# A fused attention and MLP kernel on one core: filler matmuls dealt to the first halves of slots, and one of them sent ahead of the maxima's products

## The chip, the core and the metric

The kernel runs on one core of one Trainium2 chip. A core has five engines that work side by side, each through its own queue in program order: TensorE (PE; its weight loads are shown apart as PEld), VectorE (DVE), ScalarE (ACT), GpSimd (POOL) and SyncE (SP), which here issues the DMAs. They wait for each other by semaphores. The metric is the device time of one execution in microseconds (us); less is better.

## The reference

The input x is 2048 rows of 512. It is normalised, and feeds a causal sliding-window attention (32 heads of 16, window 256) and an MLP whose SiLU gates the attention's output:

```python
xn = _layernorm(x, axis=-1)
s = _A_ref(xn, A_wqkv, A_wo)      # q, k, v; softmax(q k^T / 4 in the window) v; times wo
g = _silu(_B_ref(xn, B_w1, B_b1, B_w2, B_b2))   # layernorm, 1792 wide GELU layer, back to 512
return x + s * g
```

## The kernel before

**Layout and stages.** A preface normalises and transposes x and projects the first queries, keys and values. Then comes the attention, 128 *slots* t = 0 to 127: eight groups of four heads, and in each group 16 blocks of 128 keys. After it the rest of the MLP and the output projection follow, which the change does not touch. All matrix products in the projections are done with a high and a low part of each operand, three products in place of one.

**A slot.** The four heads of a group are kept as two pairs (p = 1 and p = 0). In slot t the loop at the end of the attention's code (from `for t in range(-16, end + 1)`) writes, in this order:

1. `prob_block(..., 1)`: scores of pair 1 into the bank pair `stb` (PE, two matmuls), exp into a tile `pt` (ACT), masks by POOL;
2. `max_block` for slot m = t + 12: products `xy` (PE, four matmuls), from which VectorE finds row maxima for a later group: a masked copy (COPY_PREDICATED) that takes parts of `zo` into `xy`, then a TENSOR_REDUCE into `mt`;
3. `fill_in(t, 0)`: the filler units of the first half;
4. `prob_block(..., 0)`: scores of pair 0 into the same `stb`, exp, masks;
5. `fill_in(t, 1)`: the filler units of the second half;
6. `first_scores` for slot m + 1: four matmuls into `zo`, which the next slot's masked copy reads (zo<-qk in the profile);
7. `closing`: where a tandem ends, ACT copies one finished bank out of PSUM, VectorE the other;
8. `pv_step`: products of exps and values (zo<-pt,vt), copied out by ACT (`oraw`).

Steps 1 to 3 are called the *first half* here, 4 to 8 the *second half*. Since there is one `stb`, the scores of either half wait for the exp of the half before. Slots 3 and 4 of each group of 16 have no first_scores, slot 5 has them with no wait for the copy; slots 14 and 15 of each 16 have narrower scores (256 and 128 columns in place of 384). In slots 1 and 2 of each 16, step 8 has 8 and 16 matmuls in place of 24.

**Fillers.** Between these steps PE does unrelated work: the projections of the next group's queries and keys, of the later heads' values (slots 51 to 73), and from slot 99 on the MLP's first layer. `tandem(t0, t1, one, two, mid)` spreads two such jobs over slots t0 to t1: a *unit* is two matmuls that run side by side on the halves of the array (64 rows each), one into `fb[0]`, one into `fb[1]`. A job pair takes 12 units of 512 columns in each of two phases (24 units of 256 columns for the values; `n` in the code, and `room` is counted in twelfths of it). `room(t, k)` says how many units half k of slot t holds, `places` deals them out. In slot t1 `closing` copies both banks out, ACT's copy and VectorE's, VectorE's behind the slot's reduction. The next tandem begins in slot t1 + 1 and its first matmul writes VectorE's bank. These are called *closing* slots (8, 13, 18, 24, 29, 34, 40, ...) and *starting* slots (9, 14, 19, 25, 30, 35, 41, ...). From slot 116 on `places_late` deals, which is left as it is. In slots 91 and 92 the fillers are transposes (`y_turn`).

Of the kernel before, what the change touches and what calls it, by code (L numbers as in the profile page):

```python
# [49 lines left out]
def mixer_kernel(ctx, tc, x, wqk, wv, wo, w1, b1, w2, b2, out):  # L50
# [106 lines left out]
    def run(steps):  # L157
        for step in steps:
            step()
# [11 lines left out]
    slots = []  # L171

    def open_slot(i):
        slots.append(bigp.tile([P, 2, 2, S], F32R, tag=f"qk{i}", name=f"qk{i}"))
# [122 lines left out]
    fills = {}  # L297
# [72 lines left out]
    def pair_qk(n, c):  # L370

        ops = [(kt, a, b) for kt in range(KT) for a, b in PASSES]
        sl = slice(512 * c, 512 * (c + 1))

        def mm(ps, i, r, **flags):
            kt, a, b = ops[i]
            nc.tensor.matmul(ps, wqs[n][r, a, kt], big[r, b, kt, sl], **flags)

        def send(src, qk, tt):
            copy_rows(slots[n % 2][tt:P:4, qk, :, sl], src[64 * qk: 64 * qk + 64])  # L380

        def finish(ps, t, copy):
            hi = sgp.tile([P, 512], F32R, tag="sh", name=f"sh_{n}_{c}", bufs=2)
            raw = t2.tile([P, 512], F32, tag="t2", name=f"pjr_{n}_{c}")
            lo = raw.bitcast(F32R)
            copy(raw, ps)

            def send_high():
                if n >= 2:
                    copy_rows(slots[n % 2][3:P:32, 0, :, sl], slots[n % 2][7:P:32, 0, :, sl])  # L390
                for qk, tt in ((1, 0), (0, 0), (1, 2), (0, 1)):
                    send(hi, qk, tt)

            def send_low():
                send(lo, 1, 1)
                send(lo, 0, 2)


            free = max(t + 1 + 2 * (c % 2), 16 * n - 28 + 4 * c)
            free += 2 * (t == 90)  # L400
            at(free, nc.scalar.copy, hi, raw)
            behind(free, send_high)
            free = quiet(max(free, t + 1))
            at(free, lambda: nc.gpsimd.tensor_tensor(lo, raw, hi.bitcast(F32), op=ALU.subtract))
            behind(free, send_low)
        return 3 * KT, mm, finish
# [37 lines left out]
    def tandem(t0, t1, one, two, mid=None, back=None):  # L444

        n = one[0]
        lo, hi = slice(0, 64), slice(64, P)
        mid = mid or max(1, (t0 + t1 + 1) // 2)  # L450
        late = t1 >= 16 * NQ - LEAD

        def room(t, k):

            m = t % 16
            if k:
                return {1: 2, 2: 1, 3: 1, 4: 1}.get(m, 0)
            return 3 if t == t0 else {5: 3, 15: 3}.get(m, 4)

        def places(slots, last):  # L460

            halves = [(t, k) for t in slots for k in (0, 1) if last or (t, k) != (mid - 1, 1)] + [(t1, 0)] * last
            units = dict.fromkeys(halves, 0)
            for _ in range(n - last * n // 12):
                h = min(units, key=lambda h: (units[h] >= room(*h) * n // 12, units[h]))
                units[h] += 1
            if last:
                units[t1, 1] = n // 12
            return [h for h in units for _ in range(units[h])]

        def places_late(slots, last):

            last = min(n // 4, n // (len(slots) + 1)) if last else 0
            cuts = [(n - last) * k // len(slots) for k in range(len(slots) + 1)]
            out = []
            for t, a, b in zip(slots, cuts, cuts[1:]):
                ahead = b - a if not last and t == slots[-1] else min(b - a, max(n // 4, (b - a + 1) // 2))
                out += [(t, 0)] * ahead + [(t, 1)] * (b - a - ahead)
            return out + [(t1, 0)] * last

        deal = places_late if late else places
        first, second = deal(range(t0, mid), False), deal(range(back or mid, t1), True)
        for phase, where in enumerate((first, second)):
            for i in range(n):
                flags = dict(start=(phase == 0 and i == 0), stop=(phase == 1 and i == n - 1), skip_group_check=True)
                def unit(i=i, phase=phase, flags=flags):
                    (two if phase == 0 else one)[1](fb[1 - phase], i, hi, **flags)
                    (one if phase == 0 else two)[1](fb[phase], i, lo, **flags)
                fills.setdefault(where[i], []).append((unit, ()))
        closing[t1] = (one[2], (fb[0], t1, nc.scalar.copy)), (two[2], (fb[1], t1, nc.vector.tensor_copy))  # L490
        if late:
            fills[t1, 0].extend(closing.pop(t1))
# [70 lines left out]
    def prob_block(n, kb, p):  # L563
        slot = slots[n % 2]
        w = min(384, S - P * kb)
        pt = pp.tile([P, 2, 384], F32, tag="pt", name=f"pt_{n}_{kb}_{p}")
        both = xy if p and 16 * n + kb + LEAD >= 16 * NQ else stb[0]
        for a in (1, 0):
            r = slice(64 * a, 64 * a + 64)
            nc.tensor.matmul(both[:, a, 0:w], slot[r, 1, p, P * kb: P * (kb + 1)],  # L570
                             slot[r, 0, p, P * kb: P * kb + w], start=True, stop=True)
        nc.scalar.activation(pt[:, :, 0:w], both[:, :, 0:w], AF.Exp, scale=DH ** -0.5)
        nc.gpsimd.affine_select(out=pt[:, :, 0:P], in_=pt[:, :, 0:P], pattern=[[0, 2], [1, P]],
                                compare_op=ALU.is_ge, fill=0.0, base=0, channel_multiplier=-1)
        if w == 384:
            nc.gpsimd.affine_select(out=pt[:, :, 256:384], in_=pt[:, :, 256:384],
                                    pattern=[[0, 2], [-1, P]], compare_op=ALU.is_gt, fill=0.0,
                                    base=0, channel_multiplier=1)
        pts[(n, kb, p)] = pt
# [100 lines left out]
    def at(t, fn, *args):  # L680
        plan.setdefault(t, []).append((fn, args))
# [71 lines left out]
    soon = {}  # L753
    tandem(3, 8, pair_qk(1, 2), pair_qk(1, 3))
    for n, spans in enumerate((((9, 13, 12), (14, 18, 17)), ((19, 24, 22), (25, 29, 28)), ((30, 34, 33), (35, 40, 38)),
                               ((41, 45, 44), (46, 50, 49)), ((74, 79, 77), (80, 84, 83)), ((85, 90, 88), (93, 98, 97))), 2):
        for c, span in zip((0, 2), spans):
            tandem(*span[:2], pair_qk(n, c), pair_qk(n, c + 1), *span[2:])
    for i, span in enumerate(((51, 56, 54), (57, 61, 60), (62, 67, 65), (68, 73, 71))):
# [61 lines left out]
    def fill_in(t, half):  # L821
        now[:] = t, half
        run(delayed.pop((t, half), ()))
        for fn, args in fills.get((t, half), ()):
            fn(*args)
# [3 lines left out]
    for t in range(-16, end + 1):  # L829
        m = t + LEAD  # L830
        if t == -5:
            open_slot(1)
            for k in range(4):
                at(-4 + k, clear_part, k)
        if 0 <= t < end:
            if t == 0:
                early.close()
                stb.append(attn.enter_context(tc.tile_pool(name="ps_s2", bufs=1, space=PSUM)).tile(
                    [P, 2, 512], F32, name="stb"))
            prob_block(t // 16, t % 16, 1)  # L840
        if t >= 0 and m < end:
            max_block(m // 16, m % 16, m in early_first)
        fill_in(t, 0)
        for fn, args in plan.get(t, []):
            fn(*args)
        if m == 1:
            max_block(0, 1)
        if 0 <= t < end:
            prob_block(t // 16, t % 16, 0)
        whole = t <= 2 or 91 <= t < 93  # L850
        if not whole:
            fill_in(t, 1)
        if t >= 0 and m + 1 < end and (m + 1) % 16 >= 2 and ((m + 1) % 4 or m >= 32):
            first_scores((m + 1) // 16, (m + 1) % 16)
            early_first.add(m + 1)
        if whole:
            fill_in(t, 1)
        if m == 0 or 1 <= m < LEAD - 1:
            max_block(0, m + (m > 0))
        for fn, args in closing.get(t, ()):  # L860
            fn(*args)
        if t >= 1:
            pv_step((t - 1) // 16, (t - 1) % 16)
        run(lns.get(t, ()))
        done = m if t >= 0 else m + 1 if 0 < m < LEAD - 1 else 0
        if done < end and done % 4 == 3:
            max_rows(done // 16, done % 16 // 4, t)
        for fn, args in ends.get(t, []):
            fn(*args)
# [20 lines left out]
    for f in range(6, NF, 2):  # L890
        t = gp.tile([P, 2, 512], F32, tag="ohl", name=f"hr_{f}", bufs=4)
# [185 lines left out]
    for c in range(2):  # L1077
# [23 lines left out]
        for i in range(NF + 1):  # L1101
# [47 lines left out]
            k = i - o_from  # L1149
# [163 lines left out]
```

## Time and profile before

| what | value |
|---|---|
| time, median of 3 runs | 750.82 us (750.6 to 752.12) |
| the profiled execution's own time | 750.51 us |
| its span on the core | 748.4 us |
| preface, attention, rest (from the timeline) | 0 to 64, 64 to 430, 430 to 748 us |
| granted TensorE clock over the span | 0.999 |

A slot takes about 2.8 us, and the attention's 128 slots half of the time. In the timeline's rows the first number is the start in us from the span's start, the second the duration, then the engine, the operation with what it writes and reads, the shapes, how many instructions are merged, and in brackets how long the engine stood idle before it and what ended that.

### The profile page before, as it was taken

The numbers are of one execution on the slowest core, as the hardware profiler recorded it, in microseconds if no ns is written. First come the engines' busy times: TensorE is split into PE (matmuls) and PEld (weight loads), VectorE is DVE, ScalarE is ACT, GpSimd is POOL, SyncE is SP. The second block draws the span as 40 slices with busy tenths as digits, with TensorE's granted clock in tenths as the row PEclk, the third lists the DMA queues.
The fourth block names the chain that finished last, engine by engine and source line by source line (L and its number), as shares of the span: only waits on it lengthen the run. The fifth ranks groups of instructions, "written<-read, shape, count | busy, mean of one in ns | idle before, by whom it ended". The sixth has DMA issues, their size and how long they took to land.

```text
span 748.4 us, 18785 instructions
## 1 busy us (share of the span) xinstructions
PE 737.2 (99%) x7412; PEld 589.7 (79%) x7412; DVE 502.5 (67%) x770; ACT 439.3 (59%) x745; POOL 314.8 (42%) x658
## 2 busy tenths in 40 slices
PE   9999999999999999999999999999999999999997
PEld 8886777777788887777776788888888888888886
DVE  8875667677677768787872648763576765676373
ACT  7756777777677666888877745454463744442001
POOL 7633777777566665867877600120102000001102
PEclk9999999999999999999999999999999999999999
DMA  8623365654348763547624482532013232253531
GB/s 284 196 61 79 73 155 146 164 141 99 95 111 250 242 220 85 134 109 201 198 76 148 136 286 94 194 122 87 26 48 103 91 99 72 69 178 120 171 95 56
DMA packets 56951, 99.40 MB, mean 133 GB/s; under 512 B 11104, under 2 KB 11360, under 8 KB 56864
## 3 DMA queue, kind: packets, MB, share of 16 engines
q1 hardware_dynamic: 56864, 98.21, 44.3%
q8 instruction: 58, 0.95, 0.5%
q14 instruction: 29, 0.24, 0.1%
HBM read 51.39 MB, written 29.62 MB: 108 GB/s over the span
## 4 chain that ended last, share of the span: by engine, by line
PE 81%; ACT 2%; DVE 1%; POOL 1%; DMA 1%; issue 1%; SPq 0%; ACTq 0%; DVEq 0%
PE acc L42 20%; PE fb L42 15%; PE zo L42 13%; PE p L42 9%; PE stb L42 9%; PE s L42 6%; PE h L42 6%; PE xy L42 3%; ACT pt L42 2%; POOL pt L42 1%; DMA qk<-mT_d 1%; PE yt L42 1%; DVE xy L42 0%; DVE mt L42 0%; SPq L42 0%
## 5 line engine op out<-in xcount | busy, mean ns | idle before, releaser
L42 POOL TENSOR_SCALAR_AFFINE_SELECT pt<-pt 128x256 f32<-128x256 f32 x480 | 189.8, 420 | 115.3 <-ACT pt L42 113.4
L42 ACT ACTIVATE pt<-stb 128x768 f32<-128x768 f32 (+1 forms) x244 | 188.6, 773 | 55.4 <-PE stb L42 47.8
L42 DVE TENSOR_REDUCE mt<-xy 128x4 f32<-128x1024 f32 (+1 forms) x128 | 152.6, 1192 | 4.4
L42 PE MATMUL acc<-w,gh 128*128 128x512 f32 x432 | 133.5, 390 | 0.0
L42 DVE COPY_PREDICATED xy<-upper,zo 128x512 f32<-128x512 int32 x112 | 77.9, 696 | 81.0 <-PE xy L42 65.8
L42 POOL TENSOR_TENSOR xo<-xo,gated 128x512 f32<-128x512 f32 x15 | 20.2, 1349 | 216.6 <-DVE gated L42 213.0
L42 PE MATMUL fb<-xnT,wqb 64*128 64x512 f32 (+1 forms) x684 | 108.2, 396 | 0.2
L42 PE MATMUL zo<-pt,vt 128*17 128x128 f32 x2880 | 103.7, 275 | 0.3 <-POOL pt L42 0.3
L42 PE MATMUL stb<-qk 64*128 64x384 f32 (+1 forms) x488 | 101.0, 409 | 2.9 <-ACT pt L42 1.3
L42 PEld LDWEIGHTS acc<-w,gh 128*128 128x128 f32 x432 | 80.8, 188 | 16.6
L42 PEld LDWEIGHTS stb<-qk 64*128 64x128 f32 x488 | 45.6, 183 | 54.8 <-ACT pt L42 46.4
L42 PE MATMUL acc<-w,gl 128*128 128x512 f32 x216 | 84.2, 390 | 0.0
L42 PEld LDWEIGHTS zo<-pt,vt 128*17 128x17 f32 x2880 | 67.5, 97 | 16.8 <-issue 7.5
L42 PEld LDWEIGHTS fb<-xnT,wqb 64*128 64x128 f32 (+1 forms) x684 | 64.9, 185 | 8.4 <-DVE pjr L42 0.8
L42 PE MATMUL xy<-qk 64*128 64x256 f32 (+2 forms) x536 | 58.2, 291 | 1.0 <-DVE mt L42 1.0
L42 ACT COPY oraw<-zo 128x128 f32<-128x128 f32 x128 | 34.3, 268 | 36.3 <-PE zo L42 35.0
L42 PEld LDWEIGHTS xy<-qk 64*128 64x128 f32 x536 | 46.8, 185 | 7.3 <-issue 3.3
L42 PEld LDWEIGHTS acc<-w,gl 128*128 128x128 f32 x216 | 40.5, 188 | 8.7 <-DVE gl L42 0.3
L42 ACT ACTIVATE gated<-acc 128x512 f32<-128x512 f32 x16 | 8.7, 596 | 63.5 <-DVE acc L42 63.5
L42 PE MATMUL s<-wos,ohl 128*128 128x512 f32 (+1 forms) x204 | 44.7, 377 | 0.0
L42 PEld LDWEIGHTS s<-wos,ohl 128*128 128x128 f32 x204 | 36.6, 188 | 7.0
L42 PEld LDWEIGHTS zo<-qk 64*128 64x128 f32 x448 | 38.4, 184 | 4.3 <-DVE xy L42 1.8
(198 smaller groups left out, 1169.2 us busy)
## 6 DMA issues: line engine op xcount, KB each, us to landing
qk<-sh SPq DMA_DIRECT2D x128, 128.0 KB
qk<-pjr SPq DMA_DIRECT2D x64, 128.0 KB
oT_d<-oraw SPq DMA_DIRECT2D x32, 256.0 KB
w_d<-in_w_dram SPq DMA_DIRECT2D x14, 512.0 KB
x<-in_x_dram SPq DMA_DIRECT2D x16, 256.0 KB
or<-oT_d SPq DMA_DIRECT2D x16, 256.0 KB
w<-rden_d SPq DMA_DIRECT2D x16, 256.0 KB
xo<-in_x_dram SPq DMA_DIRECT2D x16, 256.0 KB
```

The costliest lines, as they stand in the source:

```text
L42: r = issue(*args, **kwargs)
```

## The change

Three edits. `room` gives a first half four units (three in slot 15 of a group), also in a tandem's first slot, and a second half none but where it says 1 or 2. `places` fills the first halves before it puts anything into second halves, and takes the closing slot's two halves among them, where it used to set one unit aside for its second half. In the loop, where a slot's first half has more than one unit, its first unit is written ahead of `max_block`, so ahead of the xy products (slots 9 to 115, but for 91 and 92). One tandem's middle also moves from slot 97 to 96.

```diff
         def room(t, k):
 
             m = t % 16
-            if k:
-                return {1: 2, 2: 1, 3: 1, 4: 1}.get(m, 0)
-            return 3 if t == t0 else {5: 3, 15: 3}.get(m, 4)
+            return {1: 2, 2: 1, 3: 1, 4: 1, 15: 1}.get(m, 0) if k else {15: 3}.get(m, 4)
 
         def places(slots, last):
 
-            halves = [(t, k) for t in slots for k in (0, 1) if last or (t, k) != (mid - 1, 1)] + [(t1, 0)] * last
+            halves = [(t, k) for t in slots for k in (0, 1) if last or (t, k) != (mid - 1, 1)] + [(t1, 0), (t1, 1)] * last
             units = dict.fromkeys(halves, 0)
-            for _ in range(n - last * n // 12):
-                h = min(units, key=lambda h: (units[h] >= room(*h) * n // 12, units[h]))
-                units[h] += 1
-            if last:
-                units[t1, 1] = n // 12
-            return [h for h in units for _ in range(units[h])]
+            full = lambda h: units[h] >= room(*h) * n // 12
+            for _ in range(n):
+                units[min(halves, key=lambda h: (2, 1 - h[1], units[h]) if full(h) else (h[1], 0, units[h]))] += 1
+            return [h for h in halves for _ in range(units[h])]
...
-                               ((41, 45, 44), (46, 50, 49)), ((74, 79, 77), (80, 84, 83)), ((85, 90, 88), (93, 98, 97))), 2):
+                               ((41, 45, 44), (46, 50, 49)), ((74, 79, 77), (80, 84, 83)), ((85, 90, 88), (93, 98, 96))), 2):
...
             prob_block(t // 16, t % 16, 1)
+        if 9 <= t < 116 and t not in (91, 92) and len(fills.get((t, 0), ())) > 1:
+            fills[t, 0].pop(0)[0]()
         if t >= 0 and m < end:
             max_block(m // 16, m % 16, m in early_first)
         fill_in(t, 0)
```

How many units the halves hold, of tandems that stand for the rest (first half, second half of each slot):

| slots | before | now |
|---|---|---|
| 19 to 24 | 3,1 4,1 3,0 4,0 4,0 3,1 | 4,0 4,0 4,0 4,0 4,0 4,0 |
| 25 to 29 | 3,1 4,0 4,0 4,3 4,1 | 4,0 4,0 4,0 4,2 4,2 |
| 30 to 34 | 3,1 3,1 4,0 4,3 4,1 | 4,0 3,1 4,0 4,2 4,2 |
| 62 to 67 (half-size units) | 6,2 6,2 8,0 6,4 5,2 5,2 | 8,0 6,2 8,0 8,0 8,0 8,0 |
| 93 to 98 | 3,0 3,0 3,0 3,0 4,3 4,1 | 4,1 4,0 3,0 4,0 4,0 4,0 |

**PE's queue in slot 22**, in the middle of a tandem, before (zo<-qk are the first scores; then come the products with values):

```order
L42 MATMUL stb_890<-qk1_722 128x384 x2
L42 MATMUL xy_103<-qk0_92 128x256 x4
L42 MATMUL fb0_108<-xnT_90,wqb3_1619 128x512
L42 MATMUL fb1_109<-xnT_90,wqb3_1619 128x512
L42 MATMUL fb0_108<-xnT_90,wqb3_1619 128x512
```

and now:

```order
L42 MATMUL stb_890<-qk1_722 128x384 x2
L42 MATMUL fb0_108<-xnT_90,wqb3_1619 128x512
L42 MATMUL fb1_109<-xnT_90,wqb3_1619 128x512
L42 MATMUL xy_103<-qk0_92 128x256 x4
L42 MATMUL fb0_108<-xnT_90,wqb3_1619 128x512
```

One unit (a matmul into either bank) has moved from behind xy to ahead of it; three follow, as before. The second half is the same: stb, first scores, products.

**PE's queue from the second half of closing slot 24 into starting slot 25**, before, from stb on (the six rows of products with values between are left out by a line):

```order
L42 MATMUL stb_890<-qk1_722 128x384 x2
L42 MATMUL fb0_108<-xnT_90,wqb3_1619 128x512
L42 MATMUL fb1_109<-xnT_90,wqb3_1619 128x512
L42 MATMUL zo_104<-qk0_92 128x128 x4
...
L42 MATMUL stb_890<-qk1_722 128x384 x2
L42 MATMUL xy_103<-qk0_92 128x256 x4
L42 MATMUL fb1_109<-xnT_90,wqb3_1619 128x512
```

and now:

```order
L42 MATMUL stb_890<-qk1_722 128x384 x2
L42 MATMUL zo_104<-qk0_92 128x128 x4
...
L42 MATMUL stb_890<-qk1_722 128x384 x2
L42 MATMUL fb1_109<-xnT_90,wqb3_1619 128x512
L42 MATMUL fb0_108<-xnT_90,wqb3_1619 128x512
L42 MATMUL xy_103<-qk0_92 128x256 x4
```

The unit of the closing slot's second half is now in its first half, and the starting slot's first unit, whose first matmul writes fb1, stands ahead of xy.

**VectorE's queue over the same two slots**, the same before and now but for buffer numbers (mt are maxima, pjr a finished projection):

```order
L42 COPY_PREDICATED xy_103<-upper_115,zo_104 128x4x128
L42 TENSOR_REDUCE mt_2_4_2047<-xy_103 128x4
L42 STREAM_TRANSPOSE mT_2_0_2040<-mh_2_0_2037 128x32
L42 COPY pjr_3_1_2077<-fb1_109 128x512
L42 COPY_PREDICATED xy_103<-upper_115,zo_104 128x4x128
```

The copy that frees fb1 stands between the closing slot's reduction and the starting slot's masked copy. Nothing has moved here, nor on ACT, POOL or SP.

## The prediction

> **What bounds the kernel now.** I read the page first, for the shares and the chain that ended last.
>
> ```profile
> PE 737.2 (99%) x7412; PEld 589.7 (79%) x7412; DVE 502.5 (67%) x770; ACT 439.3 (59%) x745; POOL 314.8 (42%) x658
> ...
> PE 81%; ACT 2%; DVE 1%; POOL 1%; DMA 1%; issue 1%; SPq 0%; ACTq 0%; DVEq 0%
> ```
>
> TensorE looks full, but matmul ends are modelled and overlap, so its waits must be read from its weight loads (PEld). The view of waits for 85 to 400 us, which holds the slots that the change touches, names them:
>
> ```profile
> DVE xy L42 <- PE xy L42: 71.3, 88, 1.4
> ...
> PEld stb L42 <- ACT pt L42: 42.1, 160, 0.7
> ...
> PEld zo L42 <- DVE xy L42: 2.0, 7, 0.4
> ...
> PEld fb L42 <- DVE pjr L42: 1.2, 6, 0.3
> ...
> PEld xy L42 <- DVE mt L42: 0.4, 2, 0.2
> ```
>
> PE waits 160 times for an exp, hardly ever for the reduction ahead of an xy product (0.4 us in all), and VectorE waits 88 times for xy. So xy is late for VectorE, and VectorE is not late for xy. The timeline of slot 48 (four units in its first half, none in its second) shows why:
>
> ```profile
> 202.17 0.19 PEld L42 LDWEIGHTS stb<-qk 64*128 64x128 f32 x2 [0.21 <-issue]
> ...
> 202.45 0.40 PE L42 MATMUL xy<-qk 64*128 64x256 f32 x4
> ...
> 202.68 1.09 PE L42 MATMUL fb<-xnT,wqb 64*128 64x512 f32 x8
> 202.74 0.81 ACT L42 ACTIVATE pt<-stb 128x768 f32<-128x768 f32 x1 [0.17 <-PE stb L42]
> 202.95 0.70 DVE L42 COPY_PREDICATED xy<-upper,zo 128x512 f32<-128x512 int32 x1 [0.73 <-PE xy L42]
> ...
> 203.60 0.19 PEld L42 LDWEIGHTS stb<-qk 64*128 64x128 f32 x2 [0.26 <-ACT pt L42]
> 203.61 0.44 PE L42 MATMUL stb<-qk 64*128 64x384 f32 x2
> ...
> 203.68 1.23 DVE L42 TENSOR_REDUCE mt<-xy 128x4 f32<-128x1024 f32 x1
> 203.71 0.37 PEld L42 LDWEIGHTS zo<-qk 64*128 64x128 f32 x4
> ...
> 204.15 0.85 PE L42 MATMUL zo<-pt,vt 128*17 128x128 f32 x24
> ...
> 204.95 0.19 PEld L42 LDWEIGHTS stb<-qk 64*128 64x128 f32 x2 [0.23 <-ACT pt L42]
> ```
>
> The first half is 203.60 - 202.17 = 1.43 and ends with the exp, even with four units. The second is 204.95 - 203.60 = 1.35: first scores (zo<-qk) at 203.71, which may not overwrite zo before the masked copy (COPY_PREDICATED) has read it, at 202.95 + 0.70 = 203.65; then 24 products with V; then stb. So **two chains end together**: the exp's, and xy, masked copy, first scores, products, stb. The second has 0.06 us to spare. A unit takes (203.61 - 202.68)/4 = 0.23.
>
> **The change part by part.** All other engines' queues (ACT, DVE, POOL, SP) keep their order, so no copy, cast or DMA is moved past another, and nothing is added or removed. Only PE's order differs, in slots 3 to 115. I sum over these, against the profiled execution: span 748.4, own time 750.51, 0.3 under the median 750.82.
>
> *A. xy one unit later.* The masked copy follows xy directly (VectorE waited 0.73 for it), so it ends at 203.65 + 0.23 = 203.88 and first scores load at 203.93 instead of 203.71. What that costs, slot 54 shows, where the masked copy was late by itself:
>
> ```profile
> 220.24 0.70 DVE L42 COPY_PREDICATED xy<-upper,zo 128x512 f32<-128x512 int32 x1 [1.18 <-PE xy L42]
> ...
> 220.53 0.19 PEld L42 LDWEIGHTS stb<-qk 64*128 64x128 f32 x2
> ...
> 220.99 0.30 PEld L42 LDWEIGHTS zo<-qk 64*128 64x128 f32 x4 [0.27 <-DVE xy L42]
> ...
> 221.36 0.85 PE L42 MATMUL zo<-pt,vt 128*17 128x128 f32 x24
> ...
> 222.13 0.19 PEld L42 LDWEIGHTS stb<-qk 64*128 64x128 f32 x2 [0.21 <-issue]
> ```
>
> First scores load 0.05 after the copy's end; the products follow 0.37 behind, and stb 0.77 after that: 1.14 from load to stb. In slot 48 that gives 203.93 + 1.14 = 205.07, 0.12 to 0.13 later than 204.95. No other work covers it: PE has nothing between stb and first scores there. I count 22 slots that have no second-half unit afterwards and had none before: 22 x 0.13 = **+2.9**. (Slots of the V projection, 51 to 73, have half-size units and lose about nothing; slots 86, 102 and 103, whose masked copy was late anyway, nothing.) Between 0 and 0.23 a slot bounds it: 0 to 5.1.
>
> *B. Narrow slots.* In the last two slots of each group of 16 the scores are narrower, the exp shorter, and first scores already wait for the masked copy. Slot 31:
>
> ```profile
> 154.58 0.70 DVE L42 COPY_PREDICATED xy<-upper,zo 128x512 f32<-128x512 int32 x1 [0.70 <-PE xy L42]
> ...
> 155.33 0.30 PEld L42 LDWEIGHTS zo<-qk 64*128 64x128 f32 x4
> ...
> 156.48 0.19 PEld L42 LDWEIGHTS stb<-qk 64*128 64x128 f32 x2 [0.21 <-issue]
> ```
>
> 155.33 is 0.05 after the copy: the whole 0.23 passes on. Five such slots, one more with half-size units, and two of the other width: 7.5 x 0.23 = **+1.7**.
>
> *C. Units moved to first halves.* From closing slot 24 into starting slot 25, and from slot 28 (three units in its second half):
>
> ```profile
> 133.27 0.19 PEld L42 LDWEIGHTS stb<-qk 64*128 64x128 f32 x2 [0.21 <-ACT pt L42]
> ...
> 134.70 0.19 PEld L42 LDWEIGHTS stb<-qk 64*128 64x128 f32 x2 [0.49 <-ACT pt L42]
> ...
> 134.78 1.23 DVE L42 TENSOR_REDUCE mt<-xy 128x4 f32<-128x1024 f32 x1
> ...
> 136.05 0.65 DVE L42 COPY pjr<-fb 128x512 f32<-128x512 f32 x1
> 136.26 0.19 PEld L42 LDWEIGHTS stb<-qk 64*128 64x128 f32 x2 [0.21 <-ACT pt L42]
> ...
> 136.75 0.53 PEld L42 LDWEIGHTS fb<-xnT,wqb 64*128 64x128 f32 x6
> ...
> 137.69 0.19 PEld L42 LDWEIGHTS stb<-qk 64*128 64x128 f32 x2 [0.41 <-ACT pt L42]
> ...
> 139.25 0.19 PEld L42 LDWEIGHTS stb<-qk 64*128 64x128 f32 x2 [0.21 <-ACT pt L42]
> ```
>
> ```profile
> 146.19 0.19 PEld L42 LDWEIGHTS stb<-qk 64*128 64x128 f32 x2 [0.24 <-ACT pt L42]
> ...
> 148.20 0.19 PEld L42 LDWEIGHTS stb<-qk 64*128 64x128 f32 x2 [0.21 <-issue]
> ```
>
> A second half takes 1.35 with no unit, 1.56 with one (134.70 to 136.26), 2.01 with three. A first half of three units waits 0.49 for the exp, so a fourth there is free. One unit less saves 0.21, but A takes 0.13 back: slots 24, 40, 90, 104 gain 0.08 each; 56, 69, 73 (V units) 0.2 each, 58 0.1: **-1.0**. Ten slots go from three to two or fewer (-2.3), nine from one to two (+2.1): **-0.2**. Slot 3 now holds four units behind a late xy: **+0.2**.
>
> *D. Starting slots, the largest term.* The first unit of a tandem overwrites a bank that VectorE copies out behind its reduction in the closing slot: copy until 136.70, unit's load at 136.75. Until now xy went ahead of this wait; now xy waits in the queue behind the unit, and with it the other three units, stb, exp. Slot 25: the reduction and so the copy end 0.23 later, the closing slot gets 0.08 shorter, so the unit loads 0.49 + 0.31 = 0.80 into slot 25. A unit that was held costs more than 0.23, which slot 93 shows:
>
> ```profile
> 332.77 0.53 PEld L42 LDWEIGHTS fb<-xnT,wqb 64*128 64x128 f32 x6 [0.26 <-DVE xnT L42]
> ...
> 333.57 0.34 PE L42 MATMUL stb<-qk 64*128 64x384 f32 x2
> ```
>
> Three units in 0.80, so 0.34 for the held one. stb then comes at 0.80 + 0.34 + 0.23 (xy) + 3 x 0.23 = 2.06 instead of 1.43: +0.63; the second half goes from 1.56 to 1.48: net +0.55. By the same steps: slots 9, 25, 41, 57, 68, 74, 80, 99, 105 about 0.55 each (5.0); 14, 30, 46, 110 0.45 and 62 0.24, their closing slots being longer (2.0); 19, 35, 51 0.43 (1.3); 85 nothing, its closing slot growing with the copy's delay; 93, behind the transposes' copies, 0.8. Sum **+9.1**. Bounds: 0 if the wait does not hold xy back, 19 x 0.65 = 12.4.
>
> The Trainium skill, "TensorE: Matmul & The Clock Gate", section "The mechanism", says that weight loads may be pulled ahead but matmuls start and end strictly in program order. By that rule xy cannot pass the held unit, as D has it; were it otherwise, D would be 0. The rows above have no such case.
>
> Sum: 2.9 + 1.7 - 1.0 - 0.2 + 0.2 + 9.1 = 12.7. 750.5 + 12.7 = **763**.
>
> **The rivals.**
> *Only A to C.* The held unit turns out to cost little (the copy ends sooner, or stb is still bounded by the exp): 3.6 us, 754. Against it: slot 25 has 0.41 us to spare before its stb, and the held unit comes 0.31 later with xy and a fourth unit (0.46) newly behind it. 10%.
> *No change.* The same matmuls run, PE is busy 99% of the span, so their order is immaterial: 750.5. Against it: the 42.1 us of waits for exps. 8%. The Trainium skill, "Perfetto Trace Analysis", section "Identifying the Most-Contended Engine", calls matmul busy time no good measure and points to weight loads; here they stand at 79%, which speaks against this rival too.
> *Faster.* xy's delay is hidden (first scores do not really wait for the masked copy, and copies free the banks earlier), and only the moved units count: 0.21 in some 15 second halves, 3 us, 747.5. It decides from first scores loading before the masked copy ends; slots 31 and 54 speak against it. 5%.
> My own forecast holds 77%.
>
> **How the numbers follow.** Forecast 763. With D at 4.8 (19 x 0.25), A and B at half and C at -1.0, the low end is 750.5 + 6.1 = 756.6; with D at 12.4 and A at 5.1, 750.5 + 18.2 = 768.7. Taking in the first rival for eight in ten, 753.5 to 768. 0.2% (1.5 us) is about what a measurement of this kernel can tell from no change. Slower 0.87, same 0.08, faster 0.05.
>
> **What would show it.** Right: the wait of fb's loads for VectorE's copies rises from 1.2 us to several, with xy loads behind it; zo's loads wait for VectorE's masked copy in some 30 slots, not 7; slot 48's kind lasts 2.91 instead of 2.78; starting slots about 3.5 instead of 2.96; after slot 116 the same durations as before. Wrong: xy loading ahead of a held unit, or second halves still at 1.35 behind a later masked copy.

## The result

The changed kernel took 762.18 us (761.8 to 762.67, 4 runs), the kernel before 750.79 (750.6 to 752.12, 4 runs) beside it: a ratio of 1.0151, 95% interval 1.014 to 1.0163. It is **slower by 1.5%**, 11.4 us; the forecast was 763.0 in 753.5 to 768.0.

### The profile page after: what moved, and what is told of

Read it like the earlier page. It is cut to its first block, busy times and chain, and to the rows that moved or that the text cites. A ratio compares the mean times of both kernels' runs of the same rounds, so it can differ in the third digit from the quotient of the medians.

```text
span 759.9 us, 18783 instructions
## 1 busy us (share of the span) xinstructions
PE 742.1 (98%) x7412; PEld 588.0 (77%) x7412; DVE 502.4 (66%) x770; ACT 439.3 (58%) x745; POOL 314.9 (41%) x658
## 4 chain that ended last, share of the span: by engine, by line
PE 50%; POOL 1%; DVE 1%; ACT 1%; issue 1%; DMA 0%; SPq 0%; DVEq 0%; ACTq 0%
PE acc L42 20%; PE p L42 9%; PE s L42 6%; PE h L42 6%; PE fb L42 4%; PE zo L42 3%; PE stb L42 1%; POOL pt L42 1%; PE xy L42 1%; ACT pt L42 1%; PE yt L42 1%; DVE xy L42 1%; DMA qk<-qk 0%; DVE hr L42 0%; POOL pjr L42 0%
## 5 line engine op out<-in xcount | busy, mean ns | idle before, releaser
L42 PE MATMUL fb<-xnT,wqb 64*128 64x512 f32 (+1 forms) x684 | 116.1, 398 | 2.4 <-DVE pjr L42 1.7
L42 PE MATMUL stb<-qk 64*128 64x384 f32 (+1 forms) x488 | 99.0, 401 | 3.7 <-ACT pt L42 1.9
L42 PEld LDWEIGHTS zo<-qk 64*128 64x128 f32 x448 | 35.5, 185 | 14.8 <-DVE xy L42 10.0
L42 PE MATMUL zo<-qk 64*128 64x128 f32 x448 | 43.9, 273 | 1.2 <-DVE xy L42 0.6
```

The costliest lines, as they stand in the source:

```text
L42: r = issue(*args, **kwargs)
```

## The profile after

The page of the changed kernel, its line of busy times by engine:

```profile
PE 742.1 (98%) x7412; PEld 588.0 (77%) x7412; DVE 502.4 (66%) x770; ACT 439.3 (58%) x745; POOL 314.9 (41%) x658
```

The same instructions, and almost the same busy times, in a span of 759.9 us in place of 748.4. Nothing here tells where 11.5 us went. The view of waits from 85 to 410 us (waited in total, times, longest) does; of the kernel before, the figures of the prediction's view from 85 to 400 us stay the same to 410:

```profile
DVE xy L42 <- PE xy L42: 78.2, 90, 1.2
...
PEld stb L42 <- ACT pt L42: 35.4, 136, 0.6
...
PEld zo L42 <- DVE xy L42: 12.2, 42, 0.6
...
PEld fb L42 <- DVE pjr L42: 5.3, 12, 0.7
...
PEld fb L42 <- DVE vt L42: 1.7, 3, 0.6
...
PEld fb L42 <- DVE hr L42: 1.2, 3, 0.6
```

First scores (zo) now wait 42 times for the masked copy, 12.2 us in place of 2.0, and the loads of units (fb) wait 8.2 us for VectorE's closing copies (pjr, vt, hr) in place of 1.6. The scores' wait for the exp fell from 42.1 to 35.4: what PE loses, it loses to VectorE, and the exp chain has slack in its stead. Slot 48 of the changed kernel in the timeline:

```profile
207.00 0.19 PEld L42 LDWEIGHTS stb<-qk 64*128 64x128 f32 x2 [0.21 <-issue]
...
207.11 0.19 PEld L42 LDWEIGHTS fb<-xnT,wqb 64*128 64x128 f32 x2
...
207.29 0.42 PEld L42 LDWEIGHTS xy<-qk 64*128 64x128 f32 x4
...
208.01 0.69 DVE L42 COPY_PREDICATED xy<-upper,zo 128x512 f32<-128x512 int32 x1 [0.95 <-PE xy L42]
...
208.43 0.19 PEld L42 LDWEIGHTS stb<-qk 64*128 64x128 f32 x2 [0.26 <-ACT pt L42]
...
208.76 0.30 PEld L42 LDWEIGHTS zo<-qk 64*128 64x128 f32 x4
...
209.91 0.19 PEld L42 LDWEIGHTS stb<-qk 64*128 64x128 f32 x2 [0.21 <-ACT pt L42]
```

The first half lasts 1.43 as before. The copy ends at 208.70, first scores load 0.06 later, and the second half is 1.48 in place of 1.35; the slot 2.91 in place of 2.78. And the start of slot 25, behind closing slot 24:

```profile
137.42 0.18 PEld L42 LDWEIGHTS stb<-qk 64*128 64x128 f32 x2 [0.21 <-ACT pt L42]
...
137.52 0.65 DVE L42 COPY pjr<-fb 128x512 f32<-128x512 f32 x1
...
138.22 0.18 PEld L42 LDWEIGHTS fb<-xnT,wqb 64*128 64x128 f32 x2 [0.62 <-DVE pjr L42]
...
138.33 0.42 PEld L42 LDWEIGHTS xy<-qk 64*128 64x128 f32 x4
138.56 0.40 PE L42 MATMUL xy<-qk 64*128 64x256 f32 x4
...
138.79 0.86 PE L42 MATMUL fb<-xnT,wqb 64*128 64x512 f32 x6
...
139.05 0.70 DVE L42 COPY_PREDICATED xy<-upper,zo 128x512 f32<-128x512 int32 x1 [0.88 <-ACT pt L42]
139.26 0.19 PEld L42 LDWEIGHTS stb<-qk 64*128 64x128 f32 x2
139.49 0.34 PE L42 MATMUL stb<-qk 64*128 64x384 f32 x2
...
139.80 0.30 PEld L42 LDWEIGHTS zo<-qk 64*128 64x128 f32 x4 [0.35 <-DVE xy L42]
...
140.95 0.19 PEld L42 LDWEIGHTS stb<-qk 64*128 64x128 f32 x2 [0.21 <-ACT pt L42]
```

The held unit loads 0.05 after the copy's end at 138.17, 0.80 into the slot; xy, which needs nothing of that copy, stands behind it until 138.33. From the unit's load to the next slot's stb it is 2.73: 0.11 to xy's load, 0.72 to the masked copy, 0.70 for it, 0.05 to first scores, 1.15 to stb. The slot takes 3.53.

## The experiments

Slots are compared by the time from one first half's stb load to the next one's, in the profiled execution of each kernel.

**Fills or lead.** Four kernels split the change. *Without the lead:* the changed kernel less the two lines in the loop.

```diff
-        if 9 <= t < 116 and t not in (91, 92) and len(fills.get((t, 0), ())) > 1:
-            fills[t, 0].pop(0)[0]()
```

> The changed fills without the unit ahead of xy. My theory (the loss comes from xy standing behind that unit, terms A, B and D; moving units, term C, is worth about -1): 750 us, from 749 to 751; slot 48 back at 2.78 to 2.80, slot 25 at about 2.9 to 3.0, the weight loads of zo waiting for VectorE's copy in about 7 slots. Rival (four units in a starting slot's or a closing slot's first half are what makes the loss): 758 to 762, with starting slots still near 3.5.

Measured 749.85 us, ratio 0.9983 (0.9975 to 0.9992). The fills alone are no loss, rather a gain of 0.08 to 0.25%; slots 25 and 48 take 2.97 and 2.78 there.

*The lead on the old fills:* the kernel before with those two lines.

> The old fills with a first unit ahead of xy. My theory: 763 (761 to 765): A and B cost in every slot with four units and no second-half unit, D in the starting slots. Rival (the lead costs only together with the new fills): 751 to 755.

Measured 764.14 us, ratio 1.0178 (1.0165 to 1.0192). So the lead makes the whole loss, with either fills.

*The lead everywhere but in the 19 starting slots, and in these alone:*

```diff
-        if 9 <= t < 116 and t not in (91, 92) and len(fills.get((t, 0), ())) > 1:
+        if 9 <= t < 116 and t not in (91, 92) + STARTS and len(fills.get((t, 0), ())) > 1:
```

```diff
+        if t in STARTS and len(fills.get((t, 0), ())) > 1:
```

> As the changed kernel, but in the 19 starting slots xy goes ahead of all units as before. My theory: terms A to C only, 754 by hand (753 to 757): the starting slots drop from about 3.5 to about 3.0 (some 9 us less than the changed kernel in all), slot 48 stays at 2.90. Rival (the held first unit delays nothing that counts, since the unit waits for VectorE's bank wherever it stands, and A is most of the loss): 760 or more.

> As the changed kernel, but only the 19 starting slots send a unit ahead of xy. My theory: D alone over the moved units, 757 (755 to 760), with slot 48 at 2.79 and slot 25 at about 3.4; less than D's full 9 us over the run without any lead, because the closing slot's reduction, and with it the copy that the unit waits for, comes 0.23 earlier. Rival (A is most of the loss): 751 to 753. If the terms add up, this run's loss and that of the run with the lead everywhere but in the starting slots sum to the whole change's 11.4 within 1 us, less what the earlier copy saves.

Measured 756.43 us (ratio 1.0074, 1.0059 to 1.0089) and 755.09 us (1.0056, 1.0042 to 1.007). The first came out 2.4 above the hand's 754, the second 1.9 below 757. By groups of slots, in us against the kernel before, slots 0 to 114:

| slots, and the prediction's term | predicted | changed | no lead | lead, not in starts | lead in starts alone |
|---|---|---|---|---|---|
| A, 22 | +2.9 | +2.66 | +0.11 | +2.67 | -0.02 |
| B, 8 | +1.7 | +1.68 | -0.02 | +1.68 | +0.01 |
| C, 24, 40, 56, 58, 69, 73, 90, 104 | -1.0 | -1.37 | -0.95 | -0.94 | -1.01 |
| C, ten with a unit less | -2.3 | -2.54 | -2.40 | -2.51 | -2.35 |
| C, nine with a unit more | +2.1 | +2.06 | +2.08 | +2.06 | +2.08 |
| slot 3 | +0.2 | -0.06 | -0.06 | -0.05 | -0.05 |
| D, 19 starting slots | +9.1 | +8.85 | +0.39 | +1.65 | +6.27 |
| the rest | 0 | +0.11 | +0.55 | +0.60 | +0.29 |
| sum | +12.7 | +11.39 | -0.30 | +5.17 | +5.20 |

A and B follow the lead in their own slots, to some 0.1 us a group. D has two sources: over the run without lead, a lead in the starting slots gives 6.27 - 0.39 = 5.9, a lead elsewhere 1.65 - 0.39 = 1.3. I put this down to the closing slots, since their lead makes the closing copy later: in slot 19 it ends 0.58 into the slot, without leads 0.33. Both together give 8.5, 1.3 more than the sum; that a later copy counts more where xy is behind it is my reading of this. Of the 0.39 that the fills alone give, slots 80 and 93 have +0.22 and +0.45, the others -0.28 in sum. Slot 25 with the lead elsewhere shows xy going ahead of the same held unit:

```profile
136.56 0.19 PEld L42 LDWEIGHTS stb<-qk 64*128 64x128 f32 x2 [0.21 <-ACT pt L42]
...
136.66 0.65 DVE L42 COPY pjr<-fb 128x512 f32<-128x512 f32 x1
136.68 0.36 PEld L42 LDWEIGHTS xy<-qk 64*128 64x128 f32 x4
...
136.84 0.40 PE L42 MATMUL xy<-qk 64*128 64x256 f32 x4
...
137.34 0.69 DVE L42 COPY_PREDICATED xy<-upper,zo 128x512 f32<-128x512 int32 x1
137.37 0.75 PEld L42 LDWEIGHTS fb<-xnT,wqb 64*128 64x128 f32 x8 [0.33 <-DVE pjr L42]
137.37 1.18 PE L42 MATMUL fb<-xnT,wqb 64*128 64x512 f32 x8
```

The unit again waits for the copy (0.33), but xy is out at 0.12, the masked copy runs meanwhile, and the slot takes 1.60 + 1.46 = 3.06 in place of 3.53. The Trainium skill, "TensorE: Matmul & The Clock Gate", section "The mechanism", has matmuls in strict program order; the two slots 25 agree, since the matmuls of xy start 0.34 behind those of the held unit where they are written behind them (138.22, 138.56), and 0.53 ahead of them where they are written ahead (136.84, 137.37).

**A heavier dose of A.** Two units ahead of xy where a first half has four, not in starting slots:

```diff
+            for _ in range(2 if len(fills[t, 0]) == 4 else 1):
+                fn, args = fills[t, 0].pop(0)
+                fn(*args)
```

> As the run without a lead in the starting slots (756.4), but where a first half has four units, two of them go ahead of xy. My theory of A (after the first unit the spare time is used up, so each further unit ahead of xy passes on whole, 0.23 a slot in some 22 slots, and again in the narrow ones with four units): 762 (760 to 764), slot 48 at 3.13. Rival (a lead costs a fixed amount for breaking the order, whatever its length): 756 to 757.5.

Measured 764.79 us, ratio 1.0192 (1.0176 to 1.0207), a little above my range. Group A stands at +7.74 in place of 2.67: 5.07 / 22 = 0.23 a slot, a unit's whole time, after 0.12 for the first. My range had counted A and the narrow slots alone; the starting slots lost another 1.7, the closing slots 24, 40, 90 and 104 some 0.9. The rows of the timeline for slot 48:

```profile
207.39 0.18 PEld L42 LDWEIGHTS stb<-qk 64*128 64x128 f32 x2 [0.21 <-issue]
...
208.63 0.70 DVE L42 COPY_PREDICATED xy<-upper,zo 128x512 f32<-128x512 int32 x1 [1.18 <-PE xy L42]
...
208.82 0.19 PEld L42 LDWEIGHTS stb<-qk 64*128 64x128 f32 x2 [0.26 <-ACT pt L42]
...
209.38 0.30 PEld L42 LDWEIGHTS zo<-qk 64*128 64x128 f32 x4 [0.37 <-DVE xy L42]
...
210.53 0.19 PEld L42 LDWEIGHTS stb<-qk 64*128 64x128 f32 x2 [0.21 <-issue]
```

The first half is still 1.43, the masked copy 0.23 later than with one lead, the slot 3.14. The order as such costs nothing; the copy's delay does, from the point where the slack of 0.1 us is used up. Slot 11 shows the same from the other side: it has four units and the same leads, but by the loop's condition no first scores (nor have slots 7 and 15, beside 3 and 4 of each 16). Its masked copy ends 1.47 into the slot in the kernel before, 1.70 with one lead, 1.94 with two, and the slot takes 2.76, 2.75 and 2.77.

**A heavier dose of D.** A second small copy (128 of the 512 columns, again into the same place) ahead of VectorE's closing copy, in 16 closing slots, 14 of them right ahead of a starting slot; in the changed kernel, and in the kernel before:

```diff
+        def by_parts(o, i):
+            if n == 12 and not late:
+                nc.vector.tensor_copy(o[:, 0:128], i[:, 0:128])
+            nc.vector.tensor_copy(o, i)
...
-(two[2], (fb[1], t1, nc.vector.tensor_copy))
+(two[2], (fb[1], t1, by_parts))
```

> The changed kernel with a second, small copy (128 of 512 columns, some 0.25 us by its shape) ahead of VectorE's closing copy, in 16 closing slots, so that the bank comes free later; 14 of them stand right before a starting slot. My theory of D (the starting slot's first unit, and xy behind it, wait for that copy): the added time passes on whole, 14 x 0.25 = 3.5 us: 765.7 (764.5 to 766.5), slot 25 at about 3.75. Rival (the starting slots lose by the changed order of units itself, or by the exp, and the copy is only the last that ended): 762 to 763.

> The same small copy ahead of the closing copy in the kernel before. My theory: xy goes ahead of the held unit there, and the first half has some time to spare before its exp ends, so that at most half of the added time counts: 751.5 (750.5 to 753). Rival (a held unit costs the same wherever xy stands): 754 or more.

Measured 766.16 us (ratio 1.0207, 1.0191 to 1.0222) and 753.37 us (1.0037, 1.0023 to 1.005). The small copy took 0.27 us, and in slot 25 of the changed kernel the held unit came 0.32 later (the two copies stand merged in one row):

```profile
138.71 0.19 PEld L42 LDWEIGHTS stb<-qk 64*128 64x128 f32 x2 [0.21 <-ACT pt L42]
...
138.81 0.97 DVE L42 COPY pjr<-fb 128x128 f32<-128x128 f32 x2
...
139.83 0.19 PEld L42 LDWEIGHTS fb<-xnT,wqb 64*128 64x128 f32 x2 [0.94 <-DVE pjr L42]
...
142.58 0.19 PEld L42 LDWEIGHTS stb<-qk 64*128 64x128 f32 x2 [0.21 <-ACT pt L42]
```

From the unit's load to the next slot it is 2.75 again. In the changed kernel each of the 14 slots grew by 0.31 to 0.35, 4.65 in all: the wait passes on whole. In the kernel before they grew by 3.0, two thirds of it, where I had said at most half; slots 25, 41 and 105 by 0.07 to 0.09, but nine of the others by 0.23 to 0.30 and slot 9 by 0.33. I had read the spare time in slot 25 and carried it over to all; most starting slots have little. So neither theory holds whole: where xy goes ahead of the unit a third of the delay is saved, not half, and the rival (the same cost wherever xy stands) misses that third. The two kernels differ in their fills too, three units in place of four in these first halves, so the third is not shown to be xy's place alone.

**First scores behind the products, a miss.** If first scores wait for the masked copy, the 24 products could be done meanwhile. Tried in the changed kernel, in the one without lead, and in the kernel before:

```diff
-        if t >= 0 and m + 1 < end and (m + 1) % 16 >= 2 and ((m + 1) % 4 or m >= 32):
-            first_scores((m + 1) // 16, (m + 1) % 16)
-            early_first.add(m + 1)
...
         if t >= 1:
             pv_step((t - 1) // 16, (t - 1) % 16)
+        if t >= 0 and m + 1 < end and (m + 1) % 16 >= 2 and ((m + 1) % 4 or m >= 32):
+            first_scores((m + 1) // 16, (m + 1) % 16)
+            early_first.add(m + 1)
```

> The changed kernel with the first scores written behind the products with values, so that PE has the 24 products to do while the masked copy ends. My theory of A and B (the later masked copy stops PE only because first scores stand ahead of everything else in the second half): the 4.3 us of A and B vanish, slot 48 is back at 2.79, the loads of zo hardly wait for VectorE's copy (12.2 us before); closing slots get shorter by 0.12, so that about 1 us goes back to D: 757 (756 to 759). Rival (A and B are not that wait but a later exp or a full PE): 761 to 763.

> The changed fills, no unit ahead of xy, and first scores behind the products. My theory: the waits for the masked copy that the kernel before has too (about 2 us in narrow slots) go: 748.5 (747 to 750). Rival (the products then wait for ScalarE's copy of the same bank, or the masked copy becomes late for the next slot's xy): 750 to 753.

> The kernel before with first scores behind the products alone. My theory: 749 (747.5 to 750.5), by the same 1.5 to 2 us. Rival as in the run above: 751 to 754.

Measured 797.1, 794.64 and 799.1 us (ratios 1.0623, 1.059 and 1.065, each within 0.0018). All of my figures were wrong by 40 to 50 us, and the rivals' by 34 to 48, though the rival of the last two runs had the right kind of wait. The timeline of the kernel before with this edit, a second half:

```profile
206.08 0.69 DVE L42 COPY_PREDICATED xy<-upper,zo 128x512 f32<-128x512 int32 x1 [1.30 <-PE xy L42]
206.73 0.19 PEld L42 LDWEIGHTS stb<-qk 64*128 64x128 f32 x2 [0.25 <-ACT pt L42]
...
207.10 0.57 PEld L42 LDWEIGHTS zo<-pt,vt 128*17 128x17 f32 x24 [0.18 <-issue]
...
207.22 0.81 ACT L42 ACTIVATE pt<-stb 128x768 f32<-128x768 f32 x1 [0.53 <-PE stb L42]
208.02 0.27 ACT L42 COPY oraw<-zo 128x128 f32<-128x128 f32 x1
...
208.34 0.30 PEld L42 LDWEIGHTS zo<-qk 64*128 64x128 f32 x4 [0.67 <-ACT oraw L42]
```

Products and first scores write different columns of one bank (`otb` is `zo[:, 1, 256:384]`). Now first scores wait for ScalarE to copy the products out of it, and that copy stands behind the exp, which ends at 208.03. From 62 to 430 us the loads of zo wait 92 times, 64.7 us in all, for that copy, where the kernel before has 0.4; the waits of stb for the exp fell from 46.4 to 30.6. In PE's queue the products besides carry a wait for VectorE that they do not have in the kernel before, where first scores take it for them:

```
L42 MATMUL zo<-pt_6_0_3571,vt 17x128 [waits DVE_49]
...
L42 MATMUL zo<-qk_92 128x128 [waits Activation_49]
```

So neither of the two can cover the other: the program's waits guard the bank as a whole. The Trainium skill, "PSUM — Partial Sum Buffer", section "PSUM bank collisions raise a hardware error", has as its rule that PSUM is guarded with semaphores by bank and quadrant, or simply by bank, and not by address. The waits here agree with it. As a test of A these runs tell nothing; the doses above do.

**A version that beats both.** The run without lead gained less than its groups promised. Slots 65 and 69 took 3.46 and 3.75 us there, and the timeline shows why for the first:

```profile
246.41 0.56 SPq L42 DMA_DIRECT2D qk<-mT_d  x1
...
253.09 0.44 PE L42 MATMUL stb<-qk 64*128 64x384 f32 x2 [1.10 <-DMA qk<-mT_d]
```

The row maxima travel through SP's queue, 16 KB issued among the 512 KB copies of the MLP's weights (`stage_in`, one a slot from 55 to 70), and PE waits for them until 6.7 us after their issue. In the kernel before, the wait in slot 69 is 0.3 us; in the changed kernel, which gets there later, there is none. So I kept the fills, led one unit only in slots 12, 20, 36 and 100, where the lead had come out shorter, and spread the weights' copies:

```diff
-        if 9 <= t < 116 and t not in (91, 92) and len(fills.get((t, 0), ())) > 1:
+        if t in (12, 20, 36, 100) and len(fills.get((t, 0), ())) > 1:
...
-        behind(55 + k, stage_in, kind, j)
+        behind(55 + 2 * k, stage_in, kind, j)
```

> The changed fills with a lead only in slots 12, 20, 36 and 100, where the runs without leads in the starting slots came out shorter than those without any (about 0.3 us in all), and with the 512 KB copies of the MLP's weights issued in every second slot instead of in each. My theory: the run without leads lost 1.6 us in slots 65 and 69, where the scores waited for a transfer of the maxima (qk<-mT_d) that is queued behind those weights; with fewer in the queue both waits go: 748 us (747 to 749). Rival (the transfer is late for another reason, or the wait moves to another slot): 749.5 to 751.

Measured 751.79 us, ratio 1.0014 (1.0004 to 1.0023). Slots 65 and 69 fell to 2.78 each, but the copies, now running until slot 85, made the next group's keys late; slot 84 took 7.08 in place of 3.05. A row of that kernel:

```profile
306.16 0.69 PE L42 MATMUL xy<-qk 64*128 64x128 f32 x4 [2.42 <-DMA qk<-sh]
```

```diff
-        behind(55 + 2 * k, stage_in, kind, j)
+        behind(55 + 4 * k // 3, stage_in, kind, j)
```

> As the run before (four leads, the changed fills), but the weights' copies issued in three of four slots, from 55 to 75 instead of 85. My theory: the waits of slots 65 and 69 stay away, and slot 84, which lost 4 us to a transfer of keys (qk<-sh) behind those copies, comes back to about 3.05, so that the time is 751.8 - 4.0 = 748 (747 to 749). Rival (three in four is still too dense for the maxima's transfer, or too late for the keys): 749.5 to 751.

Measured **747.57 us** (746.9 to 747.94), ratio 0.9955 (0.9942 to 0.9969): faster than both. Slots 65 and 69 stay at 2.78 and 2.77, slot 84 is back at 3.12, and the view of waits over 62 to 430 us names no wait of TensorE for a transfer. Of the 2.4 us that its profile gained over the run without lead, slots 65 and 69 make 1.7 and the four leads 0.4. The waits for DMAs in it, the first of them a new one of ScalarE for weights that now arrive later:

```profile
ACT hf L42 <- DMA w<-w_d: 2.7, 1, 2.7
...
POOL pt L42 <- DMA qk<-sh: 0.6, 1, 0.6
...
POOL pt L42 <- DMA qk<-pjr: 0.2, 1, 0.2
```

## Why the prediction was right, and where it was off

- **What bounds the kernel.** Right: two chains, the exp's and xy's. The 0.06 us between them was too small and did not enter the sum. By the same rows the chain of xy would have reached stb in slot 48 at 203.71 + 1.14 = 204.85, 0.10 ahead of the 204.95 that the exp set, and that is the slack which the runs show: moving xy 0.23 back cost 0.12 a slot in the mean (0.06 to 0.15), a second unit the full 0.23.
- **A** (+2.9, measured +2.66) and **B** (+1.7, +1.68) are shown by the runs: they come with a lead in their own slots and go without it, and A grows with the dose.
- **C** gained more than forecast: -1.2 predicted, -1.85 measured (-1.37, -2.54, +2.06). 0.4 of it is slot 69, whose wait of 0.3 us for the maxima's transfer vanished once the kernel was slower; I had not read that row. **Slot 3** does not lose the 0.2: the exp covers its fourth unit. The rest, put at nothing, came to +0.11, but as a sum: +0.23 in slot 86, +0.11 in slot 54 and +0.10 in slot 15, against -0.15 in slot 20 and smaller ones.
- **D** (+9.1, +8.85) is right as a mechanism, in its sum, and in its steps for slot 25. The unit loads 0.80 into the slot, the matmuls of xy start 0.34 behind it, those of the three units 0.23 behind xy, and those of stb at 139.49, 2.07 into the slot (2.06 forecast); the next stb comes 1.46 after that (1.48 forecast), 3.53 in all. Counted by stb's weight load, as the slots before were, the halves look otherwise, 1.84 and 1.69, because this load comes 0.23 ahead of its matmuls, where in slot 48 of the kernel before the two start together (203.60, 203.61). Two things were not foreseen. A part of D, 1.3 of it directly, belongs to the leads outside the starting slots, and 0.39 to the fills. So *Only A to C*, the rival at 754, was 2.4 too low for the run that it describes, and 1.3 of this is that part.
- **The rivals.** *No change* and *Faster* fell with the first run: the same matmuls, 11.4 us apart. What would show each step came out as told, save that first scores wait in 42 slots, not some 30, and that about 3.5 holds only for starting slots such as 9, 25, 41 and 105; the 19 rose from 2.83 to 3.29 in the mean.

## What to carry to other kernels

Before work is sent ahead of an instruction, ask who waits for that instruction, and whether the work itself can be held: TensorE took its matmuls in written order here, and handed both delays to everything behind. Slack of a slot is read from the two chains that end it, not from busy shares, which here moved by a point or two while 11 us were lost. And a kernel made faster at one place runs into transfers that were just in time: look at the DMA waits of the faster version before the gain is booked.

## What the runs showed of the hardware beyond the forecast

- Accesses by different engines to separate columns of one PSUM bank were ordered against each other by the program's waits: swapping two groups of matmuls on one bank cost the kernel before 48.6 us, with PE waiting 0.67 us for ScalarE's copy in a slot.
- A transfer of 16 KB issued on the queue that carries 512 KB copies was awaited 6.7 us after its issue. The Trainium skill, "DMA: Bandwidth & Descriptors", section "Queues, rings and completion order", says that each DMA engine takes the descriptors of one such queue in ring order; that thinning the copies removed the wait agrees with it.
